# A recurrence and two MoE layers on one core: new priorities and due times for a list scheduler, half of the second layer's weights converted later, two more staging tiles

## The chip, the cores and the metric

One core of a Trainium2 chip runs the kernel. The metric is the device time of one execution in microseconds; the median of several runs is compared. Beside the runs there is one profiled execution, from which all rows below come.

## The reference

The kernel computes a recurrence over 768 steps for 4 x 8 heads of 40 dimensions, and sends its output through two layers that the code calls MoE (each is a plain two-layer network, 320 to 2048 to 320, over 3072 tokens):

```python
for t in range(768):                      # state: [B, H, 40, 40]
    y[:, :, t] = einsum('bhd,bhde->bhe', r[t], state)
    Sa = einsum('bhde,bhe->bhd', state, a[t])
    state = state * w[t] - einsum('bhd,bhe->bhde', Sa, b[t]) + einsum('bhd,bhe->bhde', v[t], k[t])
x = y.transpose(0, 2, 1, 3).reshape(3072, 320)
h = x @ w_in;  x = where(h > 0, h, exp(min(h, 0)) - 1) @ w_out      # first MoE
h = x @ w_in2; out = maximum(0.01 * h, h) @ w_out2                  # second MoE
```

The four weight matrices arrive as 64-bit floats. The kernel takes their raw bits and makes 32-bit floats of them on the chip.

## The kernel before

**Stages.** The recurrence runs in 12 chunks of 64 tokens (`NCH`), each for two halves `u` of the heads. `Attn.pre` loads a chunk's inputs (`W`, `AQ`, `KB`), forms running products of the decays by two scans (`Z`, `R`), scales `AQ` and `KB` with them, and makes the pair products and the transposed keys (`KBT`) on TensorE. `Attn.solve` inverts small triangular systems on VectorE (31 steps of a product and a sum, `tmp` and `TX`). `Attn.post` brings the inverse back from DRAM into `TT`, transposes it on VectorE (the tile `T1`, written `T` in the rows) and multiplies by `BO` on TensorE: `ps<-T,BO` is the first product of a solved chunk. `Attn.seq` does the sequential part (`Q`, `V`, `VU`, `S`, `GH`); its last products are `GH,KBT`. Its output goes through DRAM (`yd`) into `moe1_chunk`, which has 8 groups of products per chunk: `ph<-xs,wina` (x by w_in), the activation on ScalarE and VectorE (`e`, `gh`, `gl`: a value split into a rounded part and a rest), and `po<-gh,wouta`. The result goes to DRAM (`x2a`, `x2b`), and after the last chunk `moe2_chunk` does the same 12 times with `winb` and `woutb`.

**Weights.** `Moe.f32` loads a tile of 64-bit values, and converts it in five steps: an absolute value on ScalarE, a maximum (`tensor_scalar_max`) on VectorE or GpSimd, and three bit operations on VectorE, of which one is a `TENSOR_SCALAR` and two are `SCALAR_TENSOR_TENSOR`. Each of the two layers has 44 such tiles, in 8 groups of 5 or 6 (`Moe.parts`). For the first MoE `Moe.load` converts them at the start of the run, and splits each into a rounded part and a rest: a copy (ScalarE or VectorE) and a subtraction (VectorE or GpSimd). For the second one `Moe.convert` converts all 44 during the recurrence, through the one tile `raw` into the one tile `wf`, and stores them in DRAM (`fin`, `fout`). The tiles for the second layer's weights lie in the space of the recurrence's tiles (the pool "late" opens when the last operation on the pool "early" is done); then `Moe.load_f32` reads the 32-bit weights back through four tiles `w3` and splits them into `winb`, `wrb` and `woutb`.

**What sets the order.** `Program` is a list scheduler that runs when the kernel is built. Every operation is recorded with a priority and with the engines that may do it; `schedule` simulates the engines by its own cost model and takes, again and again, the operation that can start first, and among those the one of the lowest priority. The order on every engine's queue comes from this and is fixed in the program; an engine waits at an instruction whose inputs are not there. All instructions are issued by `issue`, so nearly all rows bear its line, L403. The numbers that steer it are `KEYS` (one row of due times for each half `u`, by step of the recurrence, relative to the chunk's `c * T`), `CB, CS` (first MoE's weights), `MO, MS, MJ` (first MoE's chunks), `VB, VS` (conversion of the second layer), `LB, LS` (its loading), `RELD` (the first `V` loads), `SLACK` (how much later an engine may end and still get an operation that another could do), and `MIX, DENSE` (an operation with dense products is preferred on TensorE while the products counted in an interval of 3.41 us are behind `MIX` times a linear target). A transfer counts as landed 1000 ns after its bytes have passed.

Of the kernel before, what the change touches and what calls it, by code (L numbers as in the profile page):

```python
# [9 lines left out]
F32 = mybir.dt.float32  # L10
# [107 lines left out]

SLACK = dict(gpsimd=180.039, scalar=394.0, vector=1.0)
RANK = dict(gpsimd=0, scalar=1, vector=2, tensor=0, sync=0)  # L120
# [9 lines left out]

MIX, DENSE = 1.22, 262.0


class Program:
# [130 lines left out]
    def schedule(s):  # L265
# [24 lines left out]
        while avail:  # L290
# [58 lines left out]
            if e == "sync":  # L349
                t[e] = st + 530.0  # L350
                xfer = max(st + 1250.0, xfer) + ns
                o.end = xfer + 1000.0
            elif e == "tensor":
# [69 lines left out]
class Moe:  # L423
# [13 lines left out]
    def f32(s, n, *loads):  # L437
# [3 lines left out]

        p = s.p
        names, flt = s.stage[s.n >= s.early]
        w = p.tile(names[s.n % len(names)])
        w = w.rearrange({3: "p a b -> p (a b)", 4: "p a b c -> p (a b c)"}[len(w.idx.shape)]) if len(w.idx.shape) > 2 else w
        w = w.bitcast(U32)[:, 0 : 2 * n]
        o = p.tile(flt[s.n % len(flt)])
        o = o.rearrange("p a b -> p (a b)") if len(o.idx.shape) > 2 else o
        o = o.bitcast(U32)[:, 0:n]
        s.n += 1  # L450
# [27 lines left out]

    def load(s, prio):

        p = s.p
        for f in range(NF // 2):
            p.prio = prio(f)
# [22 lines left out]

    def convert(s, fin, fout, prio):

        p = s.p
        for f in range(NF // 2):  # L510
            p.prio = prio(f)
# [10 lines left out]

    def load_f32(s, fin, fout, prio):
        p = s.p
        for f in range(NF // 2):
            p.prio = prio(f)
# [139 lines left out]
class Attn:  # L666
# [190 lines left out]
    def load(s, c, u):  # L857
# [4 lines left out]
        for x in range(2):  # L862
            a0 = 64 - 64 * x
            p.dma(s.V[u][a0 : a0 + 64, x].rearrange("p k h e -> p k (h e)"), s.vt[c, u, a0 : a0 + 64].unsqueeze(1).to_broadcast([64, 2, D]), 164e3)
        p.prio = s.key(c, u, 5)
# [86 lines left out]

CB, CS = -5.565, 7.664
MO, MS, MJ = 1.485, 1.001, 0.78

VB, VS, LB, LS = 3.443, 1.338, 12.789, 2.301

# [5 lines left out]
KEYS = [  # L963
    [-50.348, -62.048, -42.2, -40.0, -17.671, -12.843, -10.2, 8.971, 24.972],
    [-46.875, -34.39, -46.0, -16.695, -16.8, 12.004, 11.2, 12.3, 18.723],
]
# [7 lines left out]
def rwkv_moe_kernel(tc, xk, xr, vt, sq, sv, w_in1, w_out1, w_in2, w_out2, out):  # L974
# [11 lines left out]
    g("w3", [P, 3, 256], F32, 4, "late", fifo=False)  # L986
    g("raw", [P, 512], F32, 1, fifo=False)
    g("fin", [D, DFF], F32, 1, "dr")
# [7 lines left out]
    for n, sh, k in (  # L996
        ("idf", [P, P], 1), ("ck", [P, 4 * NCH + 1], 1), ("mask", [P, C], 1), ("sgn", [P, 2], 1),
        ("AQ", [P, 2, H, C], 4), ("KBT", [P, 2, H, E], 4), ("BT", [P, H, C], 2), ("BO", [P, H, 32], 4), ("TT", [P, H, C], 2), ("V", [P, 2, 2, H, E], 2),
        ("S", [P, H, E], 2), ("P64", [P, H], 4), ("W", [P, H * (C + 1) + 1], 1), ("Z", [P, H, C + 1], 1), ("R", [P, H, C + 1], 4),
        ("KB", [P, H, 2, C], 1), ("N", [P, 32, 32], 1), ("TX", [P, 16, 32], 1), ("tmp", [P, 256], 1), ("T1", [P, H, 32], 1),  # L1000
        ("Q", [P, H, E], 2), ("Y", [P, H * C], 1), ("RD", [P, H, C], 2), ("VU", [P, H, 2, C], 1), ("GH", [P, H, 2, C], 1),
    ):
        g(n, sh, F32, k, "early", n not in ("Y", "GH"))
# [15 lines left out]
    m1.load(lambda f: CB + CS * f)  # L1019
    m2 = Moe(p, w_in2, w_out2, "b", False, (None, (("raw",), ("wf",))))  # L1020
    fin, fout = p.tile("fin"), p.tile("fout")
    m2.convert(fin, fout, lambda f: (VB + VS * f) * T)
    x2d = []
# [14 lines left out]
    flag = a.in_range()  # L1038
    m2.load_f32(fin, fout, lambda f: LB * T + LS * f)
    for c in range(NCH):  # L1040
# [143 lines left out]
```

## Time and profile before

| | us |
|---|---|
| runs | 1171.96, 1173.88, 1174.08 |
| median | 1173.88 |
| profiled execution | 1170.92 |
| its span in the trace | 1169.2 |
| mean granted clock of TensorE | 0.968 of 2.4 GHz |

How to read the rows: PE is TensorE's products, PEld its weight loads, DVE is VectorE, ACT ScalarE, POOL GpSimd, SP the queue that issues the transfers. The page's first part has for each engine the busy microseconds, the share of the span and the instructions; its second part cuts the span into 40 slices, and PEclk is the granted clock in tenths. A window row has the stretch, its length, the busy time and the instructions of PE, PEld, DVE, ACT and POOL, the granted clock, the busy share of the DMA engines, and GB/s. A timeline row has an instruction's start, its duration, the engine, the line, the operation, output and inputs, shape and count, and in brackets the idle time ahead of it and what ended that. A row of groups has the same names with a count, then the busy time and the mean nanoseconds of one, then the idle time of the engine ahead of them and what ended most of it. "(+1 forms)" means that another shape is counted with it.

### The profile page before, as it was taken

How to read it: one execution, taken by the hardware profiler on the slowest of the kernel's cores; microseconds unless marked ns; L12 is line 12 of the kernel's file. 1: busy time of each engine (PE TensorE's matmuls, PEld its weight loads, DVE VectorE, ACT ScalarE, POOL GpSimd, SP SyncE). 2: the span in 40 equal slices, each digit the busy share in tenths (PEclk: the TensorE clock that was granted, in tenths of full speed). 3: DMA queues.
4: the chain of work that ended last, by engine and by line, in shares of the span. 5: the costliest groups of instructions: out<-in, count | busy, mean ns of one | idle time of the engine just before them, and what ended most of it. 6: DMA issues, size and time to landing. Idle time of an engine off the chain costs nothing.

```text
span 1169.2 us, 37563 instructions
## 1 busy us (share of the span) xinstructions
PE 1034.0 (88%) x15746; PEld 987.5 (84%) x15746; DVE 832.1 (71%) x2049; ACT 564.0 (48%) x1187; POOL 204.5 (17%) x275
## 2 busy tenths in 40 slices
PE   3326499998999999999999999989999999999997
PEld 2226489898888889888898898989999999999996
DVE  8998989896969898989798977585444444444432
ACT  5445457463645464646465544464333333333332
POOL 4233322131323131313222311020000000000000
PEclk9999689998989999999999999999999999999999
DMA  6756544453645454555555444270110111111000
GB/s 172 199 141 162 144 131 107 121 143 96 167 111 141 113 160 120 148 123 134 132 140 132 111 110 117 75 233 32 30 26 25 26 26 26 25 26 26 12 12 14
DMA packets 184591, 116.65 MB, mean 100 GB/s; under 512 B 128864, under 2 KB 158304, under 8 KB 184416
## 3 DMA queue, kind: packets, MB, share of 16 engines
q1 hardware_dynamic: 184416, 114.20, 38.3%
q8 instruction: 125, 2.05, 0.7%
q14 instruction: 50, 0.41, 0.1%
HBM read 90.81 MB, written 23.33 MB: 98 GB/s over the span
## 4 chain that ended last, share of the span: by engine, by line
PE 49%; DVE 25%; DMA 12%; ACT 5%; issue 5%; SPq 3%; POOL 0%; DVEq 0%; ACTq 0%; POOLq 0%
PE ps L403 22%; PE ph L403 20%; PE po L403 7%; DVE tmp L403 3%; DVE TX L403 3%; SPq L403 3%; DVE wf L403 2%; DMA W<-xk 2%; DMA KB<-xk 2%; DVE e L403 2%; DVE R L403 2%; DVE Y L403 2%; DVE gl L403 2%; ACT e L403 1%; DVE T L403 1%
## 5 line engine op out<-in xcount | busy, mean ns | idle before, releaser
L403 ACT ACTIVATE e<-ph 128x512 f32<-128x512 f32 x192 | 114.4, 596 | 208.2 <-PE ph L403 175.3
L403 PE MATMUL po<-gh,wouta 128*128 128x256 f32 x960 | 211.1, 302 | 2.4 <-DVE gh L403 1.7
L403 PE MATMUL ph<-xs,wina 128*128 128x256 f32 x1152 | 179.3, 293 | 6.8 <-DVE e L403 5.0
L403 DVE TENSOR_TENSOR gl<-e,gh 128x512 fp32r<-128x512 f32 x179 | 124.4, 695 | 75.2 <-ACT gh L403 73.7
L403 PE MATMUL ps<-woutb,gh 128*128 128x320 f32 x768 | 172.2, 309 | 0.4 <-ACT gh L403 0.4
L403 PEld LDWEIGHTS po<-gh,wouta 128*128 128x128 f32 x960 | 161.3, 197 | 9.4 <-DVE gh L403 2.1
L403 PE MATMUL po<-gl,wouta 128*128 128x256 f32 x576 | 167.0, 290 | 1.6 <-DVE gl L403 1.6
L403 PE MATMUL ph<-xs,winb 128*128 128x256 f32 x1152 | 168.0, 281 | 0.0
L403 PEld LDWEIGHTS ph<-xs,wina 128*128 128x128 f32 x1152 | 157.0, 198 | 9.3 <-DVE e L403 6.1
L403 ACT CAST gh<-e 128x512 fp32r<-128x512 f32 x165 | 102.3, 620 | 116.8 <-DVE e L403 78.6
L403 DVE TENSOR_TENSOR e<-ph,e 128x512 f32<-128x512 f32 x96 | 66.3, 691 | 125.6 <-ACT e L403 125.6
L403 PEld LDWEIGHTS ph<-xs,winb 128*128 128x128 f32 x1152 | 155.1, 188 | 0.0
L403 PEld LDWEIGHTS ps<-woutb,gh 128*128 128x128 f32 x768 | 123.2, 188 | 0.6 <-ACT gh L403 0.6
L403 PE MATMUL ps<-woutb,gl 128*128 128x320 f32 x384 | 118.9, 310 | 0.2 <-DVE gl L403 0.2
L403 PEld LDWEIGHTS po<-gl,wouta 128*128 128x128 f32 x576 | 114.2, 198 | 2.8 <-DVE gl L403 2.7
L403 DVE TENSOR_TENSOR tmp<-TX,N 128x126 f32<-128x126 f32 (+22 forms) x372 | 102.1, 274 | 13.7 <-POOL TX L403 5.1
L403 DVE TENSOR_TENSOR TX<-TX,tmp 128x126 f32<-128x126 f32 (+22 forms) x372 | 100.0, 269 | 4.2
L403 PE MATMUL ph<-xs,wra 128*128 128x256 f32 x384 | 79.5, 290 | 0.0
L403 PE MATMUL ph<-xs,wrb 128*128 128x256 f32 x384 | 77.2, 282 | 0.0
L403 DVE SCALAR_TENSOR_TENSOR e<-e,ph 128x512 f32<-128x512 f32 x96 | 65.4, 682 | 16.5 <-ACT e L403 15.1
L403 PEld LDWEIGHTS ps<-woutb,gl 128*128 128x128 f32 x384 | 72.0, 188 | 0.4 <-DVE gl L403 0.4
L403 PEld LDWEIGHTS ph<-xs,wra 128*128 128x128 f32 x384 | 62.2, 199 | 0.0
(167 smaller groups left out, 1712.5 us busy)
## 6 DMA issues: line engine op xcount, KB each, us to landing
KB<-xk SPq DMA_DIRECT2D x23, 512.0 KB
V<-vt SPq DMA_DIRECT2D x48, 160.0 KB
AQ<-xk SPq DMA_DIRECT2D x48, 128.0 KB
N<-scr SPq DMA_DIRECT2D x24, 256.0 KB
RD<-xr SPq DMA_DIRECT2D x48, 128.0 KB
VU<-xr SPq DMA_DIRECT2D x48, 128.0 KB
W<-xk SPq DMA_DIRECT2D x23, 260.5 KB
raw<-w_in SPq DMA_DIRECT2D x22, 256.0 KB
```

Source lines behind the costliest of these rows:

```text
L403: getattr(getattr(s.nc, e), m)(*[res(a) for a in args], **{k: res(v) for k, v in kw.items()})
```

## The change

The change has four parts.

- The scheduler's model: a transfer counts as landed 2000 ns after its bytes have passed, not 1000, an issue on SP takes 536 ns, not 530, the loads of `V` count at half the rate. `SLACK`, `MIX` and all due times get new values.
- Half of the second layer (`NV = 4` of its 8 groups, 22 of 44 tiles) is converted through DRAM as before. The other half is loaded raw into the `w3` tiles after the pool "late" has opened, is converted in the upper half of the same tile, and is split into `winb`, `wrb`, `woutb` from there, by `Moe.load` from its fifth group on.
- `raw` has two tiles, not one.
- `W` has two tiles, not one.

```diff
@@ -116,7 +116,7 @@
-SLACK = dict(gpsimd=180.039, scalar=394.0, vector=1.0)
+SLACK = dict(gpsimd=59.482, scalar=402.561, vector=1.0)
 RANK = dict(gpsimd=0, scalar=1, vector=2, tensor=0, sync=0)
@@ -128,7 +128,7 @@
-MIX, DENSE = 1.22, 262.0
+MIX, DENSE = 1.42, 262.0
@@ -347,9 +347,9 @@
             if e == "sync":
-                t[e] = st + 530.0
+                t[e] = st + 536.0
                 xfer = max(st + 1250.0, xfer) + ns
-                o.end = xfer + 1000.0
+                o.end = xfer + 2000.0
             elif e == "tensor":
@@ -440,13 +440,12 @@
         p = s.p
+        flat = lambda z: z.rearrange({3: "p a b -> p (a b)", 4: "p a b c -> p (a b c)"}[len(z.idx.shape)]) if len(z.idx.shape) > 2 else z
         names, flt = s.stage[s.n >= s.early]
-        w = p.tile(names[s.n % len(names)])
-        w = w.rearrange({3: "p a b -> p (a b)", 4: "p a b c -> p (a b c)"}[len(w.idx.shape)]) if len(w.idx.shape) > 2 else w
-        w = w.bitcast(U32)[:, 0 : 2 * n]
-        o = p.tile(flt[s.n % len(flt)])
-        o = o.rearrange("p a b -> p (a b)") if len(o.idx.shape) > 2 else o
-        o = o.bitcast(U32)[:, 0:n]
+        w = flat(p.tile(names[s.n % len(names)]))
+
+        o = w[:, 4 * P :] if flt is None else flat(p.tile(flt[s.n % len(flt)]))
+        w, o = w[:, 0 : 2 * n].bitcast(U32), o[:, 0:n].bitcast(U32)
         s.n += 1
@@ -476,10 +475,10 @@
-    def load(s, prio):
+    def load(s, prio, first=0):
         p = s.p
-        for f in range(NF // 2):
+        for f in range(first, NF // 2):
             p.prio = prio(f)
@@ -504,10 +503,10 @@
-    def convert(s, fin, fout, prio):
+    def convert(s, fin, fout, prio, n):
         p = s.p
-        for f in range(NF // 2):
+        for f in range(n):
             p.prio = prio(f)
@@ -520,9 +519,9 @@
-    def load_f32(s, fin, fout, prio):
+    def load_f32(s, fin, fout, prio, n):
         p = s.p
-        for f in range(NF // 2):
+        for f in range(n):
             p.prio = prio(f)
@@ -861,7 +860,7 @@
             a0 = 64 - 64 * x
-            p.dma(s.V[u][a0 : a0 + 64, x].rearrange("p k h e -> p k (h e)"), s.vt[c, u, a0 : a0 + 64].unsqueeze(1).to_broadcast([64, 2, D]), 164e3)
+            p.dma(s.V[u][a0 : a0 + 64, x].rearrange("p k h e -> p k (h e)"), s.vt[c, u, a0 : a0 + 64].unsqueeze(1).to_broadcast([64, 2, D]), 164e3, 180.0)
         p.prio = s.key(c, u, 5)
@@ -950,10 +949,11 @@
-CB, CS = -5.565, 7.664
-MO, MS, MJ = 1.485, 1.001, 0.78
-
-VB, VS, LB, LS = 3.443, 1.338, 12.789, 2.301
+CB, CS = 6.142, 2.266
+MO, MS, MJ = 1.417, 1.006, 1.075
+
+NV = 4
+VB, VS, LB, LS = 3.032, 1.488, 12.33, 1.653
@@ -961,8 +961,8 @@
 KEYS = [
-    [-50.348, -62.048, -42.2, -40.0, -17.671, -12.843, -10.2, 8.971, 24.972],
-    [-46.875, -34.39, -46.0, -16.695, -16.8, 12.004, 11.2, 12.3, 18.723],
+    [-50.348, -61.142, -42.2, -40.0, -42.238, -21.337, -19.972, -19.134, 24.972],
+    [-46.875, -29.548, -49.555, -23.276, -35.432, 16.344, 8.636, 12.3, 3.143],
 ]
@@ -984,7 +984,7 @@
     g("w3", [P, 3, 256], F32, 4, "late", fifo=False)
-    g("raw", [P, 512], F32, 1, fifo=False)
+    g("raw", [P, 512], F32, 2, fifo=False)
     g("fin", [D, DFF], F32, 1, "dr")
@@ -996,7 +996,7 @@
         ("AQ", [P, 2, H, C], 4), ("KBT", [P, 2, H, E], 4), ("BT", [P, H, C], 2), ("BO", [P, H, 32], 4), ("TT", [P, H, C], 2), ("V", [P, 2, 2, H, E], 2),
-        ("S", [P, H, E], 2), ("P64", [P, H], 4), ("W", [P, H * (C + 1) + 1], 1), ("Z", [P, H, C + 1], 1), ("R", [P, H, C + 1], 4),
+        ("S", [P, H, E], 2), ("P64", [P, H], 4), ("W", [P, H * (C + 1) + 1], 2), ("Z", [P, H, C + 1], 1), ("R", [P, H, C + 1], 4),
         ("KB", [P, H, 2, C], 1), ("N", [P, 32, 32], 1), ("TX", [P, 16, 32], 1), ("tmp", [P, 256], 1), ("T1", [P, H, 32], 1),
@@ -1017,9 +1017,9 @@
     m1.load(lambda f: CB + CS * f)
-    m2 = Moe(p, w_in2, w_out2, "b", False, (None, (("raw",), ("wf",))))
+    m2 = Moe(p, w_in2, w_out2, "b", False, ((("raw",), ("wf",)), (("w3",), None)), NV * 11 // 2)
     fin, fout = p.tile("fin"), p.tile("fout")
-    m2.convert(fin, fout, lambda f: (VB + VS * f) * T)
+    m2.convert(fin, fout, lambda f: (VB + VS * f) * T, NV)
     x2d = []
@@ -1036,7 +1036,8 @@
     flag = a.in_range()
-    m2.load_f32(fin, fout, lambda f: LB * T + LS * f)
+    m2.load_f32(fin, fout, lambda f: LB * T + LS * f, NV)
+    m2.load(lambda f: LB * T + LS * f, NV)
     for c in range(NCH):
```

VectorE has 2110 instructions in the new program, before 2049, and GpSimd 235, before 275 by the trace (271 of the scheduler's and four of the frame's); the products are the same.

**TensorE, where the first MoE begins.** `ph` is its accumulator, `AQ,KB` and `T,BO` (or `TT,T`, the step after it) belong to chunk 1 of the recurrence. Before:

```order
L403 MATMUL ps_127<-AQ_138,KB 64x64
L403 MATMUL ph_122<-xs_110,wina 128x256 x6
L403 MATMUL ph_122<-xs_110,wra 128x256 x2
L403 MATMUL ph_122<-xs_110,wina 128x256 x6
L403 MATMUL ph_122<-xs_110,wra 128x256 x2
L403 MATMUL ph_123<-xs_110,wina 128x256 x6
L403 MATMUL ph_123<-xs_110,wra 128x256 x2
L403 MATMUL ph_123<-xs_110,wina 128x256 x6
L403 MATMUL ph_123<-xs_110,wra 128x256 x2
L403 MATMUL ph_124<-xs_110,wina 128x256 x6
L403 MATMUL ph_124<-xs_110,wra 128x256 x2
L403 MATMUL ps_128<-T_171,BO_149 32x32 x16
```

Now:

```order
L403 MATMUL ps_130<-AQ_139,KB 64x64
L403 MATMUL ps_129<-AQ_139,KB 64x64
L403 MATMUL ps_128<-TT_152,T_173 32x32 x16
L403 MATMUL ph_123<-xs_110,wina 128x256 x6
L403 MATMUL ph_123<-xs_110,wra 128x256 x2
L403 MATMUL ph_123<-xs_110,wina 128x256 x6
L403 MATMUL ph_123<-xs_110,wra 128x256 x2
L403 MATMUL ph_124<-xs_110,wina 128x256 x6
L403 MATMUL ph_124<-xs_110,wra 128x256 x2
L403 MATMUL ps_130<-Q_174,TT_152 64x40 x2
L403 MATMUL ps_128<-TT_152,Q_174 40x64 x2
```

Of chunk 1's solve, `T,BO` stood behind three groups of the first MoE; now it and the product after it stand ahead of them, and chunk 1's `Q` and `TT` follow after the second group.

**The transfers (SP) at the change of stage**, after the last chunk of the recurrence. `w_11652` to `w_11655` and `w_11458` to `w_11461` are the four `w3` tiles, `xr` takes the inputs of a chunk of the second MoE. Before:

```order
L403 DMA w_11652<-fin 128x2x256
L403 DMA w_11652<-fin 64x256
L403 DMA w_11653<-fout 128x2x320
L403 DMA w_11654<-fin 128x2x256
L403 DMA w_11654<-fin 64x256
L403 DMA fout<-wf 128x2x64
L403 DMA w_11655<-fout 128x2x320
L403 DMA w_11652<-fin 128x2x256
L403 DMA w_11652<-fin 64x256
L403 DMA w_11653<-fout 128x2x320
L403 DMA w_11654<-fin 128x2x256
L403 DMA w_11654<-fin 64x256
L403 DMA w_11655<-fout 128x2x320
```

Now:

```order
L403 DMA w_11459<-fout 128x2x320
L403 DMA xr<-x2a_83 128x512
L403 DMA xr<-x2b_95 64x256 x2
L403 DMA w_11460<-fin 128x2x256
L403 DMA w_11460<-fin 64x256
L403 DMA w_11461<-fout 128x2x320
L403 DMA w_11458<-w_in 128x512
L403 DMA w_11459<-w_in 128x512
L403 DMA xr<-x2a_84 128x512
L403 DMA xr<-x2b_96 64x256 x2
L403 DMA w_11460<-w_in 64x512 x2
L403 DMA w_11461<-w_out 128x512
L403 DMA w_11458<-w_out 128x512
```

Where there were re-reads of 32-bit weights alone, re-reads of the first four groups are now mixed with the chunk inputs and with the loads of raw 64-bit tiles from `w_in` and `w_out`.

**VectorE at the change of stage.** `e`, `gh` and `gl` belong to the last chunk of the first MoE and the first of the second. Before:

```order
L403 TENSOR_TENSOR woutb<-w_11655,woutb 128x2x320
L403 TENSOR_TENSOR winb<-w_11652,winb 128x2x256
L403 TENSOR_TENSOR wrb<-w_11652,wrb 64x256
L403 TENSOR_TENSOR woutb<-w_11653,woutb 128x2x320
L403 TENSOR_TENSOR gl_118<-e_115,gh_116 128x512
L403 SCALAR_TENSOR_TENSOR e_114<-e_114,ph_124 128x512
L403 TENSOR_TENSOR wrb<-w_11654,wrb 64x256
L403 TENSOR_TENSOR woutb<-w_11655,woutb 128x2x320
L403 CAST gh_117<-e_114 128x512
L403 TENSOR_TENSOR xs_110<-xr,xs_110 128x3x256
L403 TENSOR_TENSOR gl_119<-e_114,gh_117 128x512
```

Now:

```order
L403 TENSOR_SCALAR w_11458<-w_11458 128x256
L403 SCALAR_TENSOR_TENSOR e_115<-e_115,ph_124 128x512
L403 TENSOR_SCALAR w_11458<-w_11458 128x256
L403 TENSOR_SCALAR w_11459<-w_11459 128x256
L403 SCALAR_TENSOR_TENSOR w_11458<-w_11458 128x256
L403 TENSOR_SCALAR w_11459<-w_11459 128x256
L403 TENSOR_TENSOR gl_119<-e_115,gh_117 128x512
L403 SCALAR_TENSOR_TENSOR w_11458<-w_11458 128x256
L403 SCALAR_TENSOR_TENSOR w_11459<-w_11459 128x256
L403 SCALAR_TENSOR_TENSOR e_116<-e_116,ph_125 128x512
L403 SCALAR_TENSOR_TENSOR w_11459<-w_11459 128x256
L403 TENSOR_SCALAR w_11460<-w_11460 128x256
```

Between the steps of the activation stood subtractions for re-read weights; now the bit operations of the conversions stand between them, two tiles at a time.

## Rows read from the trace of the kernel before

**Rows 1.** The page: busy time of each engine, and TensorE's granted clock in 40 slices.
```profile
PE 1034.0 (88%) x15746; PEld 987.5 (84%) x15746; DVE 832.1 (71%) x2049; ACT 564.0 (48%) x1187; POOL 204.5 (17%) x275
...
PEclk9999689998989999999999999999999999999999
```

**Rows 2.** Windows: the start, the middle, and the second MoE.
```profile
0.00:160.00 160.00, 73.36 (x1513) 64.41 (x1514) 141.34 (x431) 78.98 (x200) 51.00 (x83) 0.90 0.63 159
160.00:700.00 540.00, 507.23 (x10114) 474.39 (x10114) 472.67 (x1255) 296.99 (x656) 140.08 (x182) 0.97 0.51 129
800.00:1100.00 300.00, 300.00 (x2302) 299.98 (x2302) 122.79 (x177) 112.75 (x192) 2.59 (x2) 1.00 0.10 25
```

**Rows 3.** Timeline of TensorE up to the first product of the first MoE.
```profile
121.85 1.94 PE L403 MATMUL ps<-idf,KB 128*128 128x128 f32 x8 [9.63 <-DMA e<-w_in]
...
131.29 0.47 PE L403 MATMUL ps<-AQ,KB 40*64 40x64 f32 x2 [7.50 <-DVE AQ L403]
...
134.57 0.58 PE L403 MATMUL ph<-xs,wina 128*128 128x256 f32 x1
```

**Rows 4.** Groups of VectorE and GpSimd: the steps of conversion, splitting and scaling.
```profile
L403 DVE TENSOR_TENSOR gl<-e,gh 128x512 fp32r<-128x512 f32 x179 | 124.4, 695 | 75.2 <-ACT gh L403 73.7 <-issue 0.3
...
L403 DVE SCALAR_TENSOR_TENSOR wf<-raw,wf 128x256 uint32<-128x256 uint32 (+1 forms) x90 | 35.5, 394 | 0.5
L403 DVE TENSOR_SCALAR wf<-wf 128x256 uint32<-128x256 uint32 (+3 forms) x104 | 33.5, 322 | 13.6 <-ACT wf L403 12.7 <-POOL wf L403 0.3
...
L403 DVE TENSOR_TENSOR AQ<-AQ,R 64x512 f32<-64x512 f32 x37 | 29.4, 794 | 0.6
...
L403 DVE TENSOR_TENSOR wina<-wf,wina 128x256 fp32r<-128x256 f32 x8 | 3.3, 414 | 0.0
...
L403 POOL TENSOR_SCALAR wf<-wf 128x256 f32<-128x256 f32 (+1 forms) x22 | 22.0, 1000 | 123.8 <-ACT wf L403 70.9 <-DVE Y L403 30.3 <-issue 21.4
...
L403 POOL TENSOR_TENSOR gl<-e,gh 128x512 fp32r<-128x512 f32 x13 | 17.1, 1319 | 92.1 <-DVE gh L403 53.2 <-ACT gh L403 25.8 <-DVE TX L403 9.9
...
L403 POOL TENSOR_TENSOR AQ<-AQ,R 64x512 f32<-64x512 f32 x11 | 14.4, 1307 | 11.8 <-DVE R L403 9.4 <-issue 2.1
```

**Rows 5.** Timelines of GpSimd and VectorE at 72 us.
```profile
72.50 0.80 POOL L403 TENSOR_TENSOR wouta<-wf,wouta 128x256 fp32r<-128x256 f32 x1 [4.38 <-ACT wouta L403]
...
72.75 0.83 DVE L403 SCALAR_TENSOR_TENSOR Y<-raw,Y 128x256 uint32<-128x256 uint32 x1
...
74.01 0.42 DVE L403 SCALAR_TENSOR_TENSOR Y<-raw,Y 128x256 uint32<-128x256 uint32 x1
```

**Rows 6.** Timeline of TensorE: three of the five long waits for the transposes.
```profile
212.65 0.22 PE L403 MATMUL ps<-T,BO 32*32 32x32 f32 x2 [2.49 <-DVE T L403]
...
622.77 0.22 PE L403 MATMUL ps<-T,BO 32*32 32x32 f32 x2 [1.87 <-DVE T L403]
...
729.19 0.69 PE L403 MATMUL ps<-T,BO 32*32 32x32 f32 x30 [1.37 <-DVE T L403]
```

**Rows 7.** Windows of 3.41 us: the first long wait, and the stretch after it.
```profile
211.63:215.04 3.41, 2.10 (x40) 1.91 (x41) 3.25 (x10) 0.73 (x2) 0.00 (x0) 0.95 0.29 67
215.04:218.45 3.41, 3.41 (x46) 3.12 (x45) 3.05 (x12) 0.42 (x2) 0.00 (x0) 0.55 0.10 24
```

**Rows 8.** Change of stage: windows, groups of VectorE, and two waits on TensorE's timeline.
```profile
750.00:800.00 50.00, 44.88 (x401) 43.67 (x401) 37.69 (x67) 31.04 (x57) 6.38 (x4) 0.97 0.57 164
800.00:850.00 50.00, 50.00 (x394) 50.00 (x394) 20.89 (x32) 18.59 (x32) 2.59 (x2) 1.00 0.11 30
...
L403 DVE TENSOR_TENSOR woutb<-w,woutb 128x640 fp32r<-128x640 f32 x8 | 7.6, 948 | 1.5 <-ACT woutb L403 1.3
...
L403 DVE TENSOR_TENSOR wrb<-w,wrb 64x256 fp32r<-64x256 f32 x8 | 4.0, 504 | 0.4 <-ACT wrb L403 0.2
...
782.66 0.98 PE L403 MATMUL ph<-xs,wina 128*128 128x256 f32 x6 [2.40 <-DVE e L403]
...
793.92 0.98 PE L403 MATMUL ph<-xs,wina 128*128 128x256 f32 x6 [2.12 <-DVE e L403]
```

## The prediction

> **What bounds the kernel now.** I read the totals and the granted clock first, then the windows, then TensorE's own timeline. TensorE is busy 1034.0 of 1169.2 us [rows 1], and the windows say where it is not: 73.36 of the first 160 us, 507.23 of the next 540, and all of 800 to 1100 us [rows 2]. So there are three stretches. In the last one the second MoE feeds TensorE without a gap; the change moves nothing there that TensorE could wait for. In the first one TensorE waits for VectorE, which is busy 141.34 of 160 us [rows 2] with the first MoE's weight conversions, the solve and the operand scaling; the first product of the first MoE (`ph<-xs,wina`) starts at 134.57 us, at the lower of the two clocks, after waits of 9.63 and 7.50 us [rows 3]. In the middle TensorE is 94% busy, and what it loses comes in small waits in its in-order queue. From 150 to 800 us its timeline shows 51 waits, 39.7 us together; the largest family is the first product of a solved chunk (`ps<-T,BO`) waiting for VectorE's transposes, five large ones of 2.49, 1.62, 1.45, 1.87 and 1.37 us and 10.9 us in all (the first, the fourth and the last of them: [rows 6]). Each of these larger stalls is followed by a stretch at the lower clock: TensorE has 2.10 us of work in one window of 3.41 us, and in the next, where it is busy throughout, the granted clock is 0.55, near the 1.2 GHz level [rows 7]. From 200 to 800 us there are nine such falls, eleven windows of 3.41 us at 0.50 to 0.55, about 1.57 us lost in each, 17 us in all.
>
> So the time is: the start (about 135 us, VectorE's), then TensorE's work, then 40 us of waits and 17 us of half clock. The products are the same in both kernels; only the start, the waits and the clock can change. I make the sum against the profiled execution, 1170.92 us; the median of the runs is 1173.88, 2.96 us above it, and I add that at the end.
>
> **The start.** The same three engines do the same work; the new keys and the smaller allowance for GpSimd give another order. Up to the subtraction that makes the first `xs`, VectorE's order holds 369 rows before and 406 now. 35 of the additional instructions are weight conversions: four more tiles of the first MoE are through (39 of 44, not 35), and subtractions that GpSimd did are on VectorE. At the issue spacing in the timeline (0.20 us for the short ones, 0.34 us for those with two inputs, somewhat under the means in [rows 4]) that is 8.9 us. Against it: the second `W` tile ends a wait of VectorE for the load of `W`, more filler stands in front of the transposes, for which VectorE waits once, and fewer GpSimd instructions disturb VectorE: an update that takes 0.42 us alone took 0.83 us beside a GpSimd subtraction [rows 5]. The nearest price for that is 0.42 us for each of some twelve removed there, 5 us at most. Net, the first `ph` comes 0 to 9 us later, and I take 4. What TensorE gets for it: the first product and the second one of chunk 1's solve stand ahead of the first `ph` now, 1.3 us of work. Term: **+3 us** (0 to +10; no gain, since VectorE is busy for 141.34 of the 160 us already [rows 2] and gets more to do).
>
> The Trainium skill has a rule on this, in "SBUF — State Buffer", section "SBUF: two separate sides": VectorE with two inputs in SBUF, or in a two-port mode, and GpSimd take one pair of ports as an exclusive lock for a whole instruction, and the other blocks fully. By that rule, an instruction that leaves GpSimd would free VectorE for GpSimd's whole duration. [Rows 5] show half of that: 0.41 us lost beside a GpSimd instruction of 0.80 us. What the full lock would make of the time is the third rival below.
>
> **The middle.** The scheduler now counts 2.0 us from a transfer's end to its landing, not 1.0; half of the second MoE's 44 tiles leave the recurrence, and so do their stores to DRAM; 36 instructions go from GpSimd to VectorE (twelve `wf` clamps at 1.000 us there, eight `gl` at 1.319 us there and 0.695 us on VectorE, the rest of about 0.7 us each [rows 4]). For VectorE that is 22 tiles x (2 x 0.322 + 2 x 0.394) = 31.5 us less from chunk 7 on, and 12 x 0.322 + 8 x 0.695 + 13 x 0.414 + 3 x 0.79 = 17 us more over the whole run. Does it help the wait that matters? I compared, in each order, TensorE's work between the last product of one chunk's recurrence (`GH,KBT`) and the `T,BO` of the next with VectorE's work up to the transposes in front of it, both at the traced means. TensorE's lead over VectorE is -0.8 us before and +1.0 now in chunk 2 (the 2.49 us wait), 4.1 and 4.7 in chunk 3, 4.9 and 4.6 in chunk 8, 2.2 and 6.3 in chunk 9, 2.4 and 5.3 in chunk 11. So three of the five large waits shrink by 2 to 4 us, more than their length, and two stay: 10.9 us becomes about 5. Term: **-6 us** (-10.9, all gone, to +3: in chunks 4 to 6 the lead falls by 0.3 to 0.9 us).
>
> The clock follows the stalls. Of the nine falls, three hang on the waits that shrink, and the larger MIX makes the scheduler put dense products sooner into an interval that is behind. I take four falls less, at 1.57 us a window and one of them with two windows, and round down: **-7 us** (-17, none left, to +5, three more).
>
> The second `raw` tile, the rate for `V` and the 6 ns for an issue alter the order alone; their effect is in the terms above, none has a price of its own. The transfers saved (22 stores and as many re-reads) are hidden, since VectorE waits little for them.
>
> **The change of stage.** Here the moved work lands. From the last `GH,KBT` (752 us) to the first product of the second MoE (799 us), TensorE finishes the first MoE. VectorE has 12.3 us free from 750 to 800 us and 29.1 from 800 to 850 [rows 8], about 30 in the 80 us up to 830. Into that come 43 short instructions at 0.322, 44 with two inputs at 0.394 and some 23 subtractions at 0.414 us [rows 4], 13.8 + 17.3 + 9.5 = 40.6 us; four of the eight groups that came from DRAM go (4 x (0.948 + 0.504) + 2 x 0.685 = 7.2 us [rows 8]), and 5.0 us of conversions that stood there already. Net +28 us into 30 us. It just fits: in the new order TensorE has 60 us of work from the last `GH,KBT` until it needs the third quarter of the weights and 70 us until the last piece, and VectorE 30 and 61 to 67 us. ScalarE's part (22 short instructions) and the loads (22, four tiles deep, SP's queue behind them holding only later inputs and the stores of chunks 10 and 11) lie beside that. But VectorE waits in order, and TensorE already waited 2.40 and 2.12 us here for its results [rows 8], when it was this dense for 20 us, not 65. Term: **+4 us** (-5, those waits gone too; +18, if VectorE is held up a fifth of the time: 67 / 0.8 = 84 against 70, and 4 on the first MoE's own steps). If the cover is gone, all 28 us show.
>
> **Sum.** +3 - 6 - 7 + 4 = -6: 1164.9 for the profiled execution, 1168 as a median.
>
> **Rivals.**
> 1. The change of stage becomes VectorE's (slower): +18 in place of +4, 1182 us. For it: 28 us into 30, and every conversion waits for a load and for ScalarE. Against: the last piece has 3 to 9 us of lead. It decides once VectorE is under 88% busy there.
> 2. The waits only move (slower): another order has its own small stalls, as the 40 us before are spread over many pairs of engines; middle and clock at 0, 1181 us. Against: in chunks 9 to 11 the lead grows by 3 to 4 us.
> 3. More is gained: GpSimd blocks VectorE for its whole time. The moved instructions blocked it for 12 x 1.0 + 8 x 1.319 + 3 x 1.31 + 13 x 0.72 = 36 us and cost 17 on VectorE, so it is 19 us better off: start 0, waits -9, clock -13, change of stage 0, 1152 us. Against: [rows 5] show half a block. That full lock is the rule quoted above.
> 4. The change does not do what its first words say: half the gains of the middle, 1174.5 us, no difference. For it: the rhythm of TensorE's order within a chunk (products between two dependent steps) is the same in nearly every chunk.
>
> **How the numbers follow.** Forecast (1163 to 1171.5 us) 0.36; rival 1 0.17; rival 2 0.14; rival 3 0.16; rival 4 0.17. A measurement of this kernel can tell 0.2%, 2.3 us, from no change. Faster is the forecast and rival 3, 0.52; the same is rival 4, 0.17; slower rivals 1 and 2, 0.31. The range reaches from rival 3 to just above rivals 1 and 2, 1152 to 1183; the forecast's own range is 1163 to 1171.5.
>
> **What would show it.** The first `ph<-xs,wina` at 136 to 142 us; waits of `ps<-T,BO` for VectorE under 6 us in all; four to six falls of the clock between 200 and 800 us; VectorE over 90% busy for some 60 us after the last `GH,KBT`, with TensorE idle there for 8 to 10 us; TensorE without a gap from 800 to 1100 us, as before. The first `ph` after 146 us, TensorE idle over 15 us at the change of stage, or nine falls again would make it wrong.

## The result, and the profile after

The changed kernel takes 1141.2 us (median; 1137.46 to 1141.46), the kernel before 1173.7 us: a ratio of 0.9719, 95% interval 0.9696 to 0.9741. It is faster by 2.8%; the forecast was 1168, and the time lies under the range too. The profiled execution took 1141.0 us, its span is 1139.2 us.

The page's totals and granted clock of the kernel after, as [rows 1]:

```profile
PE 1023.0 (90%) x15746; PEld 979.2 (86%) x15746; DVE 837.4 (74%) x2110; ACT 562.6 (49%) x1188; POOL 157.0 (14%) x239
...
PEclk9976579999999999999999999999999999999999
```

TensorE is idle for 116.2 us of the span in place of 135.2, and busy for 11.0 us less with the same 15746 products, so the rest is the clock. The windows show where. They are cut at the first `ph<-xs,wina`, at the last `GH,KBT` and at the first `ph<-xs,winb`; I call the second one the middle. First the kernel before, then the kernel after:

```profile
0.00:134.57 134.57, 51.11 (x1136) 44.03 (x1136) 119.77 (x379) 63.20 (x164) 42.61 (x71) 0.93 0.65 163
134.57:752.13 617.56, 579.67 (x11478) 542.02 (x11475) 530.55 (x1399) 334.76 (x737) 152.88 (x198) 0.96 0.50 126
752.13:799.35 47.22, 42.09 (x379) 41.11 (x378) 35.44 (x63) 30.24 (x56) 6.38 (x4) 0.96 0.59 172
```

```profile
0.00:143.54 143.54, 56.50 (x1200) 48.91 (x1200) 132.38 (x418) 68.33 (x181) 32.20 (x62) 0.78 0.67 169
143.54:721.31 577.77, 559.15 (x11364) 524.56 (x11360) 502.27 (x1326) 317.86 (x689) 119.99 (x171) 0.98 0.48 119
721.31:769.89 48.58, 48.58 (x451) 48.19 (x451) 40.84 (x99) 34.61 (x69) 3.34 (x3) 1.00 0.53 155
769.89:1130.93 361.04, 358.75 (x2738) 357.55 (x2736) 161.91 (x270) 141.36 (x250) 1.45 (x3) 1.00 0.11 29
```

The start is 9.0 us longer, the middle 39.8 us shorter, and what follows the last `GH,KBT` as long as before. In the middle TensorE's idle time falls from 37.9 to 18.6 us; its busy time falls by 20.5 us, of which 11.8 is the clock (the busy time of each slice of 3.41 us, times what its granted clock lacks to 1, adds up to 21.0 us before and 9.2 after; counted by the exact stretches of the lower clock it is 22.3 and 9.5), and the rest is products that moved ahead of the first `ph` or behind the last `GH,KBT`. VectorE is busy in the middle for 28.3 us less. Put together: +9.0 for the start, -19.3 and -3.4 for waits in the middle and behind it, -13.3 for the clock, and some -3 for products that changed stage (the middle has 114 records less, the start 64 more), -30.0 in the span. In the start TensorE's granted clock is 0.78 in place of 0.93; what that costs is inside the +9.0.

After the first `ph`, `T,BO` still waits for more than 1 us in two chunks, 4 and 5, each time in two parts; on TensorE's timeline, as an answer to [rows 6] (chunk 5's second part, at 388.40 us, is 0.83 us):

```profile
327.04 0.24 PE L403 MATMUL ps<-T,BO 32*32 32x32 f32 x2 [1.15 <-DVE T L403]
328.18 0.69 PE L403 MATMUL ps<-T,BO 32*32 32x32 f32 x30 [0.90 <-DVE T L403]
...
387.35 0.21 PE L403 MATMUL ps<-T,BO 32*32 32x32 f32 x2 [0.92 <-DVE tmp L403]
```

At the change of stage, which answers to [rows 8], VectorE is 94% busy for 50 us, the conversions cost 0.399 and 0.285 us (forecast: 0.394 and 0.322), and TensorE waits there once, for 1.64 us (a window, two groups of VectorE from 721 to 841 us, and the one wait):

```profile
750.00:800.00 50.00, 48.25 (x393) 47.84 (x392) 46.90 (x136) 33.03 (x73) 2.75 (x4) 1.00 0.36 105
...
L403 DVE SCALAR_TENSOR_TENSOR w<-w 128x256 uint32<-128x256 uint32 (+1 forms) x44 | 17.3, 399 | 0.1
...
L403 DVE TENSOR_SCALAR w<-w 128x256 f32<-128x256 f32 (+3 forms) x43 | 12.0, 285 | 0.0
...
783.42 0.98 PE L403 MATMUL ph<-xs,winb 128*128 128x256 f32 x6 [1.64 <-DVE e L403]
```

### The profile page after: what moved, and what is told of

It is laid out like the page before. It is cut to its first block, busy times and chain, and to the rows that moved or that the text cites. A ratio compares the mean times of both kernels' runs of the same rounds, so it can differ in the third digit from the quotient of the medians.

```text
span 1139.2 us, 37489 instructions
## 1 busy us (share of the span) xinstructions
PE 1023.0 (90%) x15746; PEld 979.2 (86%) x15746; DVE 837.4 (74%) x2110; ACT 562.6 (49%) x1188; POOL 157.0 (14%) x239
## 4 chain that ended last, share of the span: by engine, by line
PE 55%; DVE 19%; issue 4%; ACT 4%; DMA 4%; SPq 1%; POOL 1%; DVEq 0%; ACTq 0%; POOLq 0%
PE ps L403 25%; PE ph L403 22%; PE po L403 8%; DVE tmp L403 2%; DVE TX L403 2%; DVE e L403 2%; DVE gl L403 2%; DVE w L403 2%; SPq L403 1%; DMA N<-scr 1%; DVE T L403 1%; DVE R L403 1%; DMA scr<-TX 1%; ACT e L403 1%; DVE AQ L403 1%
## 5 line engine op out<-in xcount | busy, mean ns | idle before, releaser
L403 PE MATMUL po<-gh,wouta 128*128 128x256 f32 x960 | 204.5, 296 | 0.0
L403 DVE TENSOR_TENSOR gl<-e,gh 128x512 fp32r<-128x512 f32 x187 | 129.9, 694 | 84.5 <-ACT gh L403 83.7
L403 PE MATMUL ph<-xs,wina 128*128 128x256 f32 x1152 | 176.9, 290 | 1.7 <-DVE e L403 1.7
L403 PE MATMUL po<-gl,wouta 128*128 128x256 f32 x576 | 163.7, 284 | 1.1 <-DVE gl L403 0.9
L403 PEld LDWEIGHTS po<-gh,wouta 128*128 128x128 f32 x960 | 156.2, 191 | 5.4
L403 PEld LDWEIGHTS po<-gl,wouta 128*128 128x128 f32 x576 | 110.7, 192 | 2.3 <-DVE gl L403 2.3
L403 DVE TENSOR_TENSOR tmp<-TX,N 128x126 f32<-128x126 f32 (+22 forms) x372 | 99.1, 266 | 13.2 <-DMA N<-scr 4.7
L403 DVE TENSOR_TENSOR TX<-TX,tmp 128x126 f32<-128x126 f32 (+22 forms) x372 | 97.2, 261 | 4.0
L403 PE MATMUL ps<-idf,KB 128*128 128x128 f32 x184 | 29.7, 305 | 42.4 <-ACT wouta L403 18.0
## 6 DMA issues: line engine op xcount, KB each, us to landing
KB<-xk SPq DMA_DIRECT2D x23, 512.0 KB
```

The source lines that it names most:

```text
L403: getattr(getattr(s.nc, e), m)(*[res(a) for a in args], **{k: res(v) for k, v in kw.items()})
```

## The experiments

Three theories. **Theory 1**: the recurrence goes at VectorE's pace, and the conversions that left it are the gain. **Theory 2**: it is the landing times in the plan. **Theory 3**: it is the new due times. Names that begin with a_ are the changed kernel with one edit undone; b_ is the kernel before with edits done alone; k_ is the changed kernel with the old due times and one more edit undone.

**a_nv8**, all 44 tiles through DRAM again:

```diff
-NV = 4
+NV = 8
```

> The changed kernel with NV = 8: all 44 tiles of the second MoE go through DRAM during the recurrence again, all else is as changed. Theory 1 (the recurrence runs at VectorE's pace, and the 22 tiles' 31.5 us that left it are the gain): TensorE's stretch from the first ph<-xs,wina to the last GH,KBT goes from 577.8 us back by 25 to 32 us, and of that 20 or more shows in the time, 1160 to 1170 us. Theory 2 (the gain is the plan's landing times, which put the instructions that wait for a transfer where it has landed): at most 8 us, under 1149. Theory 3 (the due times, found by search, are the gain): under 1149 too.

Measured: 1153.2 us, between the theories; the middle is 19.6 us longer (597.4), but after the last `GH,KBT` 5.9 us come back.

**a_land**, the old model of a transfer:

```diff
-                t[e] = st + 536.0
+                t[e] = st + 530.0
-                o.end = xfer + 2000.0
+                o.end = xfer + 1000.0
```

> The changed kernel with the old model of transfers: landing 1000 ns after the bytes (issue 530 ns), all else as changed. Theory 1: the same VectorE work, so 1141 +-4 us. Theory 2: the waits of T,BO for VectorE come back (from 3.9 to some 12 us) with the falls of the clock behind them, 1155 to 1165 us. Theory 3: an order that was searched with other landing times loses some, 1145 to 1155.

Measured: 1162.8 us, as theory 2 has it. The waits of `T,BO` are back, 18.1 us in all; the longest are longer than any before:

```profile
275.74 0.24 PE L403 MATMUL ps<-T,BO 32*32 32x32 f32 x2 [2.79 <-DVE T L403]
...
449.79 0.24 PE L403 MATMUL ps<-T,BO 32*32 32x32 f32 x2 [3.48 <-DVE T L403]
```

**b_nv4** and **b_land**, each of the two edits alone on the kernel before:

```diff
+NV = 4      (b_nv4, with the functions that take it)
-                o.end = xfer + 1000.0
+                o.end = xfer + 2000.0      (b_land, with 536 ns for an issue)
```

> The kernel before with NV = 4 alone: 22 tiles converted after the recurrence, old due times, old landing, one raw and one W tile. Theory 1: 20 to 30 us faster than before, 1144 to 1154 us, with the stretch from the first ph to the last GH,KBT at 585 to 597 instead of 617.6. Theory 2: 0 to 8 us faster. Theory 3: no gain, 1170 or more, since the due times aren't made for it.

> The kernel before with the new model of transfers alone (landing 2000 ns after the bytes, issue 536 ns). Theory 1: no gain, 1174 +-4. Theory 2: 12 to 20 us faster than before, 1154 to 1162 us, T,BO's waits at some 5 us in place of 12.8. Theory 3: no gain or slower, since the due times were chosen with the old model.

Measured: 1170.0 us (ratio 0.9977, 0.9935 to 1.0019) and 1169.8 us (0.9972, 0.9936 to 1.0008), so neither gains anything that can be told from none; theory 2, which had 12 to 20 us for b_land, does not hold by itself either. In b_nv4 the middle is 10.7 us shorter (606.9), and the stretch from there to the end 12.2 longer. Of these, 3.6 us are waits of TensorE (17.4 us after the last `GH,KBT`, before 13.9), 2.9 are clock (4.6, before 1.7), and the rest is products that left the middle. So about half of it is the first rival, with its waits at the change of stage:

```profile
805.77 0.98 PE L403 MATMUL ph<-xs,winb 128*128 128x256 f32 x6 [1.71 <-DVE e L403]
...
812.07 0.63 PE L403 MATMUL ps<-woutb,gl 128*128 128x320 f32 x1 [3.83 <-DVE gl L403]
```

In b_land the waits of `T,BO` fall from 13.3 to 9.1 us, and others take their place: TensorE's idle time in the middle is 36.4 us, before 37.9.

**b_nv4land**, both on the kernel before:

> The kernel before with both edits that gave nothing alone: NV = 4 and the new landing times; old due times, SLACK, MIX, one raw and one W tile. If the two only work together, 1145 to 1158 us. If it needs the due times, 1165 to 1175 us.

Measured: 1154.2 us, 17 less than before (0.9861, 0.9816 to 0.9905), where the two alone gave 2 each. With these due times they work only together.

**a_jit1** and **a_keys**, the accident of an order and the due times:

```diff
-    [-46.875, -29.548, -49.555, -23.276, -35.432, 16.344, 8.636, 12.3, 3.143],
+    [-46.575, -29.248, -49.255, -22.976, -35.132, 16.644, 8.936, 12.6, 3.443],      (a_jit1)
+    (a_keys: KEYS, CB to MJ and VB to LS with the old numbers, as in the diff of the change)
```

> The changed kernel with the due times of the second half of the heads (the second row of KEYS) all 0.3 us later, nothing else: another order from the same edits. It shows how much of a difference is the accident of one order. If an order's own accidents are small, 1137 to 1145 us, and the differences of 12 and 22 us on undoing NV or the landing are those edits' own. If accidents are large, 1146 to 1160 us, and neither edit's price is known to better than that.

> The changed kernel with all old due times (KEYS, CB, CS, MO, MS, MJ, VB, VS, LB, LS); NV = 4, landing 2000 ns, SLACK, MIX and the two tiles as changed. If the due times only fit the edits together (theory 3), the gain is lost, 1160 to 1170 us. If the edits carry it (theories 1 and 2), 1141 to 1152 us.

Measured: 1138.0 and 1145.0 us. Theory 3 falls: with all old due times the gain is still there (a ratio of 0.9768, 0.9729 to 0.9807), and the due times together are worth 4 us, less than the accident of one order (a_jit3, below). a_jit1 is 3 us under the changed kernel, but the two intervals (0.9666 to 0.9746 for it) cover each other: no run showed a kernel that can be told to be faster than the changed one.

**a_slack** and **b_slack**, GpSimd's allowance undone and done alone (ScalarE's, which hardly moves, goes with it):

```diff
-SLACK = dict(gpsimd=59.482, scalar=402.561, vector=1.0)
+SLACK = dict(gpsimd=180.039, scalar=394.0, vector=1.0)      (a_slack; b_slack the other way round)
```

> The changed kernel with the old SLACK (GpSimd gets work that ends up to 180 ns later than VectorE would, not 59). If work taken from GpSimd costs VectorE its own time alone, this gives VectorE 15 to 20 us back and some 9 us of an earlier start: 1130 to 1141 us. If GpSimd's instructions hold VectorE up for longer than they save it (the rival that forecast more than I did), 1146 to 1155 us.

> The kernel before with the new SLACK alone (29 instructions go from GpSimd to VectorE). If GpSimd blocks VectorE for as long as this cost on undoing it (11 us), 1158 to 1166 us. If that price is one of the whole set of edits, as with NV and the landing, which gave 2 us each alone, 1166 to 1174 us.

Measured: 1152.2 us, and 1182.1 alone on the kernel before, 0.75% slower than it (1.0043 to 1.0107) and outside both expectations: alone the edit loses 9 us, within the set it is worth 11. The page's totals say what the moved instructions cost VectorE; after is above, this is a_slack:

```profile
PE 1031.7 (89%) x15746; PEld 987.3 (86%) x15746; DVE 837.4 (73%) x2086; ACT 560.2 (49%) x1184; POOL 183.8 (16%) x267
```

VectorE has 24 instructions less than in the kernel after, and is busy for the same 837.4 us.

**a_mix**, **a_tiles** and **a_land30**:

```diff
-MIX, DENSE = 1.42, 262.0
+MIX, DENSE = 1.22, 262.0      (a_mix)
-    g("raw", [P, 512], F32, 2, fifo=False)
+    g("raw", [P, 512], F32, 1, fifo=False)      (a_tiles, and W from 2 to 1)
-                o.end = xfer + 2000.0
+                o.end = xfer + 3000.0      (a_land30)
```

> The changed kernel with the old MIX (1.22). If the larger MIX is what keeps TensorE's clock up (dense products put sooner into an interval that is behind), the falls after the first ph go from 4 to 7 or more and the time to 1147 us or more. If the clock only follows the waits, 1137 to 1145 us with 4 or 5 falls.

> The changed kernel with one raw and one W tile. My prediction gave the second tiles no price of their own: then 1137 to 1146 us. If they are what lets VectorE go on with fill-in work while a load is under way, VectorE's busy share of the middle falls under 0.85 and the time is 1150 us or more.

> The changed kernel with a landing 3000 ns after the bytes, 1000 more than now. If the gain from 1000 to 2000 ns comes because 2000 is right (the trace shows 3.5 us from a store's issue to the dependent load's, the new model has 3.6), 3000 is wrong on the other side: T,BO's waits stay at 5 us or fall, but work that could go on is put later, 1150 to 1165 us. If it is only that more lead is better, 1130 to 1142 us.

Measured: 1151.1, 1151.7 and 1157.7 us. a_mix falls between its two cases: the falls of the clock go from 4 to 5 only, but three of the five last 10.2 us, and the clock costs 18.1 us in the middle, not 9.2. With one tile the first `ph` comes 17 us sooner (126.5), and the middle is 27.9 us longer, VectorE busy in it for 20.3 us more, a share of 0.86, which is not under the 0.85 expected:

```profile
126.50:732.20 605.70, 584.29 (x11498) 547.61 (x11498) 522.54 (x1388) 329.23 (x720) 120.62 (x176) 0.94 0.47 120
```

a_land30 loses 16 us, so it is not that more lead is better. SP's timeline of the kernel before shows the chain that rests on the landing, from the stores of the solve to the loads that need them:

```profile
203.36 1.27 SPq L403 DMA_DIRECT2D scr<-TX  x2
...
207.54 1.81 SPq L403 DMA_DIRECT2D TT<-scr  x4
```

That is 4.18 us. By the code's model (a second issue after 0.53, then 1.25, then 131 KB at 360 bytes per ns, 0.36, then the landing) it is 3.14 us with 1000 ns, 4.14 with 2000 and 5.14 with 3000. (The 3.5 and 3.6 of the expectation count from the second store's issue.) This is one of nine chunks of that kernel in which SP waited for these stores to land; from the first store's issue to the landing they took 3.9 to 5.2 us, and six in the kernel after took 3.6 to 5.3. So 1000 ns puts every one of them too early in the plan, 2000 lies among them, and 3000 is too late for all but three of the fifteen.

**k_land, k_nv8, k_slack, k_mix, k_tiles** undo the same edits with the old due times, **a_jit3** moves each of the 18 `KEYS` by a random step of up to 2 us. They ask whether a price belongs to the edit or to one order.

> The changed kernel with the old due times (1145.0 us by itself) and the old landing (1000 ns). If the landing's price of 22 us is its own, 1160 to 1172 us with T,BO's waits over 10 us. If it was an accident of the new due times, 1140 to 1152 us.

> The changed kernel with the old due times and NV = 8. If the price of 12 us is the 22 tiles' own, 1153 to 1162 us, with some 20 us more in the stretch from the first ph to the last GH,KBT. If an accident, 1140 to 1150 us.

> The changed kernel with the old due times and the old SLACK. If GpSimd's instructions block VectorE for more than they save, 1151 to 1162 us, VectorE busy for longer in the middle than the 502 us of the kernel without this edit. If an accident, 1140 to 1149 us.

> The changed kernel with a random step of up to 2 us either way on each of its 18 due times (KEYS). A due time that moves by 0.3 us cost nothing (1138.0), all old ones 4 us (1145.0). If an order's accidents are about that size, 1138 to 1146 us; if they are as large as the edits' prices, 1148 us or more.

> The changed kernel with the old due times (1145.0 us by itself) and the old MIX. If MIX's price of 10 us is its own, 1151 to 1160 us. If an accident of the new due times, 1140 to 1149 us.

> The changed kernel with the old due times and one raw and one W tile. If the tiles' price of 11 us is their own, 1152 to 1162 us, with an earlier first ph and a longer middle as at the new due times. If an accident, 1140 to 1149 us.

Measured: 1161.3 us for k_land and 1157.5 for k_tiles, each in its case of an own price; 1148.4 for k_slack, the case of an accident; 1152.5 for k_nv8, between its two cases; 1166.0 for k_mix, above both; and 1151.4 for a_jit3, the case in which accidents are as large as the edits' prices.

All of it in one table: medians in us (the kernel before, measured again beside each, took 1171.2 to 1173.8); of each profiled execution the first `ph`, the length of the middle, TensorE's idle time in it (in brackets `T,BO`'s), what the clock cost there, and VectorE's busy time there. All columns but the time are of one execution; in the four executions of the kernel after, TensorE's mean granted clock went from 0.961 to 0.992, the time from 1137.5 to 1141.5.

| kernel | time | first ph | middle | idle (T,BO) | clock | VectorE |
|---|---|---|---|---|---|---|
| before | 1173.7 | 134.6 | 617.6 | 37.9 (13.3) | 21.0 | 530.5 |
| b_land | 1169.8 | 135.1 | 616.7 | 36.4 (9.1) | 22.8 | 539.4 |
| b_nv4 | 1170.0 | 132.3 | 606.9 | 34.6 (8.9) | 20.6 | 510.6 |
| b_nv4land | 1154.2 | 135.0 | 594.1 | 31.3 (8.2) | 11.5 | 519.1 |
| b_slack | 1182.1 | 131.1 | 627.8 | 43.7 (11.8) | 27.0 | 531.5 |
| **after** | **1141.2** | 143.5 | 577.8 | 18.6 (4.8) | 9.2 | 502.3 |
| a_jit1 | 1138.0 | 141.4 | 575.4 | 17.6 (4.4) | 9.3 | 499.9 |
| a_jit3 | 1151.4 | 144.9 | 586.9 | 26.1 (3.0) | 16.3 | 505.4 |
| a_land | 1162.8 | 131.1 | 603.6 | 33.9 (18.1) | 22.5 | 511.6 |
| a_land30 | 1157.7 | 153.1 | 582.9 | 24.1 (3.4) | 12.5 | 496.6 |
| a_nv8 | 1153.2 | 142.5 | 597.4 | 24.6 (7.9) | 17.1 | 522.9 |
| a_slack | 1152.2 | 130.1 | 603.7 | 32.1 (6.8) | 15.9 | 516.9 |
| a_mix | 1151.1 | 141.6 | 591.4 | 25.6 (5.6) | 18.1 | 501.0 |
| a_tiles | 1151.7 | 126.5 | 605.7 | 21.4 (2.6) | 35.2 | 522.6 |
| **a_keys** | **1145.0** | 147.9 | 577.9 | 22.4 (4.7) | 4.7 | 502.1 |
| k_land | 1161.3 | 132.9 | 604.0 | 29.4 (11.8) | 21.7 | 518.0 |
| k_nv8 | 1152.5 | 146.8 | 595.0 | 26.3 (3.0) | 14.9 | 522.2 |
| k_slack | 1148.4 | 141.7 | 590.1 | 24.6 (5.6) | 11.7 | 512.0 |
| k_mix | 1166.0 | 147.3 | 594.8 | 27.4 (9.7) | 13.3 | 505.8 |
| k_tiles | 1157.5 | 135.5 | 605.3 | 33.1 (4.8) | 12.4 | 524.3 |

The price of undoing an edit, at the new due times and at the old ones: landing 21.6 and 16.3 us; the tiles 10.5 and 12.5; MIX 9.9 and 20.9; NV 12.0 and 7.4; SLACK 11.0 and 3.3. An order's own accident is not small: a_jit3, which undoes nothing, lost 10.2 us (0.9765 to 0.9838 of the kernel before, clear of 0.9696 to 0.9741), a_jit1 gained 3.2; these two are all that was tried of it, both at the new due times. So only the landing stands clear of it at both sets by its time alone; the tiles lie just above it. The middle is 19.6 and 17.1 us longer without NV, and a_jit3's only 9.1. With one tile it is 27.9 and 27.4 longer, but it also begins 17.0 and 12.4 us sooner. The clock costs 8.9 and 8.6 us more with the old MIX; since it costs 7.1 more in a_jit3, that is not shown to be MIX's own. What SLACK gives in time stays open. The five prices at the new due times add up to 65 us, twice the gain of 32.5: the edits are not terms of a sum.

## Why the prediction was wrong, point by point

**The start** was forecast at +3 (0 to +10), and the first `ph` at 136 to 142 us. It came at 143.5, +9.0: the upper end. The table shows three edits behind it: with the old SLACK it is at 130.1, with the old landing at 131.1, with one tile at 126.5. The first I had; the second `W` tile I had with the wrong sign, as something that brings the first `ph` forward; the landing I had not. Each of the three, undone, makes the middle longer by more than the start gets shorter (25.9, 25.8 and 27.9 us).

**The waits** were forecast at -6 (-10.9 to +3) and measured at -19.3; this is the step that failed, and the only term that left its own range. `T,BO` did in sum what I worked out: from 13.3 to 4.8 us over the middle, -8.5, of which 1.9 is chunk 1's, which stands ahead of the first `ph` now. Of its five long waits, chunks 2, 9 and 11 were to shrink and did; chunks 3 and 8 were to stay, and went to 0.55 us and to nothing; what is left stands in chunks 4 and 5, where I had the lead fall by 0.3 to 0.9 us. But I let the other waits, some 24 us, stand as they were, and gave VectorE's smaller load no term of time at all outside that one family. They fell as well, from 24.6 to 13.8. What made them fall stays open. In a_nv8, where the 22 tiles are back in the recurrence, 6 us of TensorE's idle time come back, half of it at `T,BO`, and the others are 16.7; in a_land they are 15.8, in a_slack 25.3; but a_jit3, which undoes nothing, has 23.1, nearly as many as before. The second rival had the same waits merely move; b_land shows that such a thing happens, in b_land and not here.

**The clock** was forecast at -7 and measured at -11.8 in the middle and -1.5 at the change of stage. After 200 us I expected four to six falls; two are left, at 217 and 330 us. That most of it hangs on the waits, as I had it, was not tried by itself; MIX I had named without a number, and its 9 us of clock are not clear of an order's accident. One reading was wrong: not each of the larger stalls is followed by the lower clock. After the wait of 1.45 us at 563.5 us the granted clock of the kernel before stayed at 1.00 (a window of it):

```profile
566.50:570.00 3.50, 3.50 (x94) 3.20 (x96) 3.07 (x8) 0.96 (x3) 0.00 (x0) 1.00 0.20 64
```

**VectorE's added work** was forecast at 17 us, each moved instruction at its own mean. This is the second failed step. Three pairs of kernels that differ in SLACK, and by it in their order, say what became of VectorE's busy time: 24 instructions more for 0.0 us (a_slack and after), 28 more for 1.6 us less (k_slack, 842.2 us with 2082, and a_keys, 840.6 with 2110), 32 more for 2.5 us (before and b_slack, 834.6 with 2081). The traces show why. In all twenty, no VectorE instruction with nothing of GpSimd's beside it lasted more than 0.02 us above the median of its kind and shape. Beside GpSimd, 101 instructions of the kernel before lasted over 0.1 us more than that, 43.3 us in all. In b_slack this loss is 32.8 us; it is 33.9 in a_slack and 29.7 after, 40.3 in k_slack and 29.0 in a_keys. What the instructions take by themselves rose in the same pairs by 14.1, 9.5 and 10.7 us: so 4 to 11 us of what they cost came back. The third rival had the mechanism, not its size: it had 36 us of block removed and VectorE 19 us better off, and from the kernel before to the kernel after the loss fell by 13.6. One group with a block lifted is the scan `R<-W,R`, on the same 23 instructions; but SLACK alone did not lift it, for in a_slack, with the old SLACK, the mean is 1273 ns (the kernel before, then after):

```profile
L403 DVE TENSOR_TENSOR_SCAN R<-W,R 128x520 f32<-128x520 f32 x23 | 32.6, 1419 | 0.0
```

```profile
L403 DVE TENSOR_TENSOR_SCAN R<-W,R 128x520 f32<-128x520 f32 x23 | 28.8, 1253 | 0.0
```

**The change of stage** was forecast at +4 and came out at -3.4 of waits: the lead of 60 and 70 us of TensorE's work over VectorE's 30 and 67 held, with VectorE 94% busy. The bound was right, and the value should have been its lower end. With the other old settings the same edit does run into that wall, for 3.6 us of waits and 2.9 of clock (b_nv4).

**What had no price.** I wrote that the second `raw` tile, the rate for `V` and the issue time have none, and put the second `W` tile into the start alone. The two tiles together are worth 10.5 to 12.5 us, which is just above an order's accident. Which of the two, and the rate by itself, was not tried.

**The landing** I took as one of many things that alter the order. It is the edit without which NV = 4 gives nothing that can be told from none (b_nv4); undone it costs 21.6 us, alone it gives 2.

**The range.** My four lower bounds, 0, -10.9, -17 and -5, add up to -33: 1138 us for the profiled execution, which took 1141.0. The range stopped at 1152, the third rival's time, which has one of the four terms at its end. The clock and the change of stage came near their lower ends, and the waits went beyond theirs, together; that one cause, VectorE's load and a plan that knows when data lands, moves them all is my reading, not shown. Part of the miss is the luck of one order: the same edits took 1151.4 us in a_jit3, at the lower end of the range, so of the 27 us under the forecast some 10 are within what an order alone moved.

What stays open too: the cause of the correlation between VectorE's busy time in the middle and the middle's length. Over the twenty profiles a straight line has a slope of 1.0 (85 us above VectorE's time, correlation 0.85), as if VectorE set the pace throughout; but a kernel that starts its middle sooner also has more of VectorE's work in it, and no run separated the two.

## What to carry to other kernels

Look first at whether a planner's model of waiting is true to the trace (here the landing of a dependent transfer), before the work is cut: with the wrong landing the lighter VectorE gave 2 us (b_nv4), with the right one 16 (b_nv4land against b_land). When work leaves an engine on which many small waits of the bound engine end, don't price one family of waits; price them all, and the clock behind them: here the waits that I had left out fell by 10.8 us. And before any price of one reordering is believed, measure an order that changes nothing: here that alone moved the time by up to 10 us.

## What the runs showed of the hardware that I had not expected

What GpSimd relieves VectorE of, it largely takes from it again. On the timelines of the kernel before, VectorE's scan begins 0.10 us after GpSimd's subtraction, and takes 2.31 us, not the 1.23 it takes alone; first VectorE, then GpSimd, then the same scan with GpSimd quiet (56.25 us is after GpSimd's instruction at 55.53 us had ended, and ahead of its next at 58.30):

```profile
233.62 2.31 DVE L403 TENSOR_TENSOR_SCAN R<-W,R 128x520 f32<-128x520 f32 x1
```

```profile
233.52 1.30 POOL L403 TENSOR_TENSOR gl<-e,gh 128x512 fp32r<-128x512 f32 x1 [1.82 <-PE ps L403]
```

```profile
56.25 1.23 DVE L403 TENSOR_TENSOR_SCAN R<-W,R 128x520 f32<-128x520 f32 x1
```

The same happens three more times (at 413.94, 526.48 and 643.53 us), and a cast of 0.42 us took 1.52 beside a GpSimd subtraction of 1.74. So a `gl` on GpSimd cost VectorE 1.08 us here, where doing it itself costs 0.695. Not each one does: the thirteen of the kernel before cost VectorE 6.4 us together, 0 to 1.24 each and 0.49 in the mean. In sum, the moved instructions changed VectorE's busy time by 0.0, -1.6 and +2.5 us in the three pairs above. VectorE instructions that read PSUM show none of it: 133 of them ran beside GpSimd in the kernel before, none more than 0.02 us longer than alone, and `e<-e,ph` takes 682 ns in the mean before and 681 after.

The Trainium skill, on the page "SBUF — State Buffer", section "SBUF: two separate sides", tells of an exclusive lock for the whole instruction. The trace agrees here: the scan lost 1.08 of the 1.20 us that GpSimd's instruction had left. [Rows 5], from which I took half a block, were a weaker case: VectorE started 0.25 us into an instruction of 0.80, and lost 0.41 of the 0.55 us left.
